# Kernel spectra of neighbouring time blocks added by accumulating transfers for all four sequences in six of eight channel chunks, with new places in the period and behind it

## The chip, the cores and the metric

The kernel runs on one core of a Trainium2 chip. The metric is the device time of one execution in microseconds (us); lower is better. The engines of the core are named as the profile names them: PE (TensorE, matrix products), DVE (VectorE, elementwise work), ACT (ScalarE, activations and copies), POOL (GpSimd, here mostly an issuer of transfers) and SP (SyncE, the other issuer of transfers).

## The reference

Two kinds of layer alternate, twice each, over `x` of 2048 rows and 512 channels:

```python
x = A_u
x = x + _A_ref(_layernorm(x), A_re, A_im, B_re, B_im, C_re, C_im, log_dt, Dskip)
x = x + _B_ref(_layernorm(x), w_gate, w_up, w_down)
x = x + _A_ref(...)          # the same parameters again
x = x + _B_ref(...)
# _A_ref: a long convolution per channel
dt = exp(log_dt); logdA = dt * (A_re + 1j*A_im); dB = dt * (B_re + 1j*B_im)
K = einsum("dn,dnl,dn->dl", C, exp(logdA[:, :, None] * arange(2048)), dB).real
y = irfft(rfft(u padded to 4096) * rfft(K padded to 4096))[:2048] + u * Dskip
# _B_ref: (silu(x @ w_gate) * (x @ w_up)) @ w_down, with 1376 hidden features
```

The filter `K` of each of the 512 channels has to be made once, from 128 complex exponentials per channel. Both convolution layers use it.

## The kernel before

The 2048 rows are cut into four blocks of 512 (`NB`). A convolution of blocks is done in the frequency domain: block `b` of the output needs, for every `k` up to `b`, the product of the spectrum of input block `b-k` with a kernel spectrum `w[k]`. A kernel spectrum `w[k]` covers two neighbouring time blocks of the filter, so for `k` of 1 to 3 it is a sum of two parts, one from the transform of block `k` and one, turned by a sign and with real and imaginary part exchanged, from that of block `k-1`. Each spectrum is taken as four sequences `q` of 128 frequencies. `w[0]` stays on the chip in `w0r`, the other three go to DRAM (`wdr`).

The filters are made in eight chunks of 64 channels. The work of the eight chunks overlaps in a repeating **period**, about 27 us long. For chunk `c` it holds, in the order in which one chunk passes through:

- `gen_tiles`, `gen_turns`, `gen_trig`, `gen_exp`: phases, sines, cosines and exponentials, written into `wall`, which holds two chunks in turn (DVE L409, L413, L417; ACT L428 to L430, L439 to L455). `upper` (ACT L449) squares a part of them into `mu`.
- `gen_g` and `gen_e`: the two factors of the filter (DVE L475 to L505 for `g`, L462 to L468 for the exponentials). The last step of `g` is an accumulating transfer issued by POOL (L495).
- `lags` (PE L515, 256 small products into the PSUM tile `pk`), then the copy `spread_in` (ACT L526), two transfers through DRAM that turn the layout round (SP L533 and L535) into the tile `kt`, and `skip` (DVE L522), which adds the direct term.
- `spectra(c, kt, q0)`, twice: for `q0` of 0 the sequences 0 and 2, for `q0` of 1 the sequences 1 and 3. Each does 16 fp32 products (32 records in the trace) into one of two large PSUM tiles (`pbig`) and makes the sums described above.
- `sizes` (ACT L625), beside it one spectrum of the second input block (`second`: PE L317, ACT L320, SP L321) and the norms of some weight rows (`weights`: POOL L348 loads, ACT L354 squares into `sq`, PE L357 sums, DVE L360 takes the largest). The loads use three buffers in turn, and each waits for the square that read its buffer before.

The two calls of `spectra` make the sum in two ways. With `q0` of 0, ACT copies the turned part to `wo` (L572), DVE adds the direct part from PSUM (L581), and SP stores the result. With `q0` of 1, ACT copies the turned part to `wo` and the direct part to `wa` (L576, tile tag `z`, one buffer), SP stores `wo`, and POOL then adds `wa` in DRAM with an accumulating transfer (`store_w(..., G, accum_op=OP.add)`, L556), which waits until the store has landed. Both also copy `w[0]` (L577).

The order of everything in the period is written by hand: `at(t, f)` puts a step on a list with a time, the list is sorted, and all instructions of PE, DVE, ACT and POOL are issued in that order (a step at a later number stands later in each engine's row; the number itself is not a time on the chip). `starts` gives the start of chunk `c`'s period, `n` in `use` is that of the next one. `prepare` places the phases and exponentials of a chunk two ahead, `factors` those of the next one. Behind the period comes a hand-written sequence of `take(...)` and `split(...)` calls: the last chunks' spectra (`first_parts`, `later_parts`), the first convolution (`conv`, `ssm_half`) and the split of the weights into two fp16 halves (`split`: ACT L681 and L706, DVE L679, L686 and L709). The rest, from about 296 us on, are the gated layers (`ffn`) beside the other convolutions; there a scheduler in the build sets the order.

Of the kernel before, what the change touches and what calls it, by code (L numbers as in the profile page):

```python
# [33 lines left out]
NCH = D // DC  # L34
# [43 lines left out]
def kernel(ctx, tc, x, a_re, a_im, b_re, b_im, c_re, c_im, log_dt, d_skip,  # L78
                           w_gate, w_up, w_down, c_ef, c_ei, c_ek, c_am, c_eh, c_eih, out):
    nc = tc.nc  # L80
    V, A, G, PE = nc.vector, nc.scalar, nc.gpsimd, nc.tensor
# [122 lines left out]
    def direct_size():  # L204

        da = tl([1, D], "da", "sg")
        A.activation(da, dsk, AF.Abs)
        V.tensor_reduce(dmax, da, axis=AX.X, op=OP.max)
# [238 lines left out]
    def upper(ts):  # L447

        A.activation(ts[2][:, 1:], ts[0][:, 1:32], AF.Square)  # L449
# [69 lines left out]
    def skip(ch, kt, eng):  # L519

        k = kt[0:1, :, 0]
        eng.tensor_tensor(k, k, dsk[:, ch * DC:(ch + 1) * DC].rearrange("p (g d) -> p g d", g=4), OP.add)  # L522
# [35 lines left out]
    def spectra(ch, kt, q0):  # L558


        h, cq = ch // NQ, ch % NQ
        pw = pbig([P, 2, 2, NB, 4, 16], "pw")
        for j in range(2):
            products(pw[:, j], kt, 0, NB, q0 + 2 * j, [(i, c) for i in range(2) for c in range(4)])
        yield
        if q0:
            wo = spare[0][:, 16 * DC:].rearrange("p (j k i d) -> p j k i d", j=2, k=NB - 1, i=2)
        else:
            wo = tl([P, 2, NB - 1, 2, DC], "wo", "sg")
        pv = pw.rearrange("p j i k g d -> p i j k (g d)")  # L570
        for i in range(2):
            A.activation(wo[:, :, :, i], pv[:, 1 - i, :, :NB - 1], AF.Copy, scale=sgn[:, i:i + 1])  # L572
        if q0:
            wa = tl([P, 2, NB - 1, 2, DC], "wa", "z")
            for i in range(2):
                A.activation(wa[:, :, :, i], pv[:, i, :, 1:], AF.Copy)  # L576
        A.activation(w0r[:, h, q0::2, cq], pw[:, :, :, 0].rearrange("p j i g d -> p j i (g d)"), AF.Copy)  # L577
        yield
        if not q0:
            wv = wo.rearrange("p j k i d -> p i j k d")  # L580
            V.tensor_tensor(wv, pv[:, :, :, 1:], wv, OP.add)  # L581
            yield
        for j in range(2):
            store_w(h, cq, q0 + 2 * j, wo[:, j])
        yield
        if q0:
            for j in range(2):
                store_w(h, cq, q0 + 2 * j, wa[:, j], G, accum_op=OP.add)
            yield
# [33 lines left out]
    def sizes(ch, kt, junk):  # L623

        A.activation(junk, kt, AF.Abs, accum_out=wsum[:, ch:ch + 1])  # L625
# [20 lines left out]
    def take(it, n):  # L646
        for _ in range(n):
            next(it, None)
# [332 lines left out]
    ts = [None] * (NCH + 2)  # L981
# [15 lines left out]
    with tc.manual_schedule(engines={mybir.EngineType.Activation, mybir.EngineType.DVE, mybir.EngineType.PE, mybir.EngineType.Pool}):  # L997
# [14 lines left out]
        tr = gen_trig(ts[0])  # L1012
# [10 lines left out]
        ge, tn = gen_e(ts[0]), gen_turns(1, ts[1])  # L1023
# [6 lines left out]
        tr = gen_trig(ts[1])  # L1030
# [24 lines left out]
        def at(t, f, n=1):  # L1055
            plan.append((t, len(plan), (lambda: take(f, n)) if hasattr(f, "__next__") else f))

        def later(make):

            yield from make()  # L1060

        def prepare(c, t):

            def tiles():
                ts[c] = gen_tiles(c)
            at(t + 0.05, tiles)
            steps = {k: later(lambda g=g: g(c, ts[c])) for k, g in
                     (("turns", gen_turns), ("exp", gen_exp))}
            tr = later(lambda: gen_trig(ts[c]))
            at(t + 0.35, steps["turns"])  # L1070
            at(t + 0.45, tr)
            at(t + 13.0, steps["turns"], 3)
            at(t + 13.2, steps["turns"], 3)
            at(t + 17.0, tr)
            at(t + 8.3, steps["exp"], 100)

        def factors(c, t):

            at(t + 0.2, lambda: upper(ts[c]))

            def tiles(c):
                gs[c] = tl([P, 2, 32, DC], "g", ("ga", "gb")[c % 2])
            if c == 1:
                at(t + 0.1, lambda: tiles(c))
            if c + 1 < NCH:
                at(t + 8.05, lambda: tiles(c + 1))
            gg, ge = later(lambda: gen_g(c, ts[c], gs[c])), later(lambda: gen_e(ts[c]))
            for k in range(4):
                at(t + 0.2 + 2 * k, gg, 2)
            at(t + 0.3, ge)  # L1090
            for k in range(5):
                at(t + 8.2 + k, gg)
            for k in range(4):
                at(t + 22.0 + 0.6 * k, ge, 1 if k < 3 else 100)

        def use(c, t):

            box, kt, n = {}, kt2[:, c % 2], starts[c + 1]

            def copy():  # L1100
                box["ks"] = spread_in(box["pk"])
                if c < NCH - 2:
                    spread(c, box["ks"], kt)
            at(t, lambda: box.update(pk=lags(ts[c], gs[c])))
            at(t + 7.1, copy)
            if c == NCH - 2:
                at(t + 10.0, lambda: spread_pe(c, box["ks"], kt))
            if c < NCH - 2:
                at(t + 13.1, lambda: skip(c, kt, V))
            at(t + 25.0, lambda: sizes(c, kt, box["ks"]))  # L1110
            for q0, ats in list(enumerate(((t + 17.5, t + 25.2, n + 2.1, n + 7.5),
                                      (n + 6.9, n + 14.0, n + 17.3, n + 21.0))))[:2 if c < NCH - 2 else 1]:
                sp = later(lambda q0=q0: spectra(c, kt, q0))
                if c == NCH - 2:
                    tail["sp"] = sp
                    ats = ats[:2]
                for t0 in ats:
                    at(t0, sp)

        def second_block(k, t):  # L1120
            box = []
            at(t - 3.0, lambda: box.append(second(*sec[k])))
            at(t + 14.0, lambda: take(box[0], 1))
            at(t + 17.6, lambda: take(box[0], 1))

        def weights(n, t0, t1, t2, t3):

# [19 lines left out]
        for i in range(NCH - 1):  # L1147
            t = starts[i]
            use(i, t)
            factors(i + 1, t)  # L1150
            second_block(i, t)
            if i + 2 < NCH:
                prepare(i + 2, t)
            for k, t0, t1, t2, t3 in ((0, -13.0, 0.25, 13.9, 22.3), (1, 0.3, 14.5, 17.45, 22.9),
                                      (2, 15.0, 26.5, 28.05, 36.0)):
                n = ((3, 3, 0), (3, 3, 0), (3, 3, 0), (3, 2, 0), (3, 2, 0), (3, 3, 0), (3, 3, 3))[i][k]
                if i == NCH - 2 and k == 2:
                    t0, t1, t2, t3 = 15.0, 20.0, 24.0, None
                if n:
                    weights(n, t + t0, t + t1, t + t2, t3 and t + t3)  # L1160
        t = starts[NCH - 1]
# [8 lines left out]
        c, kts = NCH - 1, (kt2[:, 0], kt2[:, 1])  # L1170
# [15 lines left out]
        def split(hi, lo, load=0):  # L1186
            for _ in range(load):
                loads.pop(0)()
            for _ in range(hi):
                his.pop(0)()  # L1190
            for _ in range(lo):
                los.pop(0)()
# [9 lines left out]
        conv = [ssm_half(0, 0, h) for h in range(2)]  # L1202
# [7 lines left out]
        ks = spread_in(pk)  # L1210
        odd = later_parts(c - 1, kts[0], (1, 3))
        rest = later_parts(c, kts[1])
# [4 lines left out]
        last = second(*sec[-1])  # L1217
# [15 lines left out]
        first_parts(c, 2)  # L1233
        take(conv[0], 1)
        split(1, 0)
        take(conv[1], 1)
        take(last, 1)
        take(last, 1)
        split(0, 1)
        split(0, 0, 1)  # L1240
        take(conv[1], 1)
        take(conv[0], 1)
        take(conv[1], 1)
        split(1, 0)
        split(1, 0)
        split(0, 0, 1)
# [8 lines left out]
        take(conv[1], 1)  # L1255
        take(odd, 1)
        direct_size()
        take(norm, 1)
        take(rest, 1)
        take(rest, 1)  # L1260
        take(odd, 1)
        take(conv[1], 1)
        take(rest, 1)
        take(odd, 1)
        take(block1, 1)
        take(rest, 1)
        split(1, 0)
        take(norm, 1)
        take(norm, 1)
        take(odd, 1)  # L1270
        take(rest, 1)
        split(0, 1)
        take(rest, 1)
        split(1, 0)
        take(rest, 1)
        split(0, 1)
        take(conv[0], 1)
        take(rest, 1)
        split(1, 0)
        take(rest, 1)  # L1280
        split(0, 1)
        split(0, 0, 1)
        split(0, 0, 1)
        take(rest, 1)
        split(0, 0, 1)
        take(rest, 1)
        sizes(c, kts[1], ks)
        take(rest, 1)
        nn2 = tl([P, 2, D], "nn2", "nn")
        nt3 = sb.tile([P, D], F16, name="nt3")  # L1290
        parts = itertools.cycle([nn2[:, 1].bitcast(F16)[:, i * D:(i + 1) * D] for i in range(2)] + [nt3])
# [54 lines left out]
```

## Time and profile before

| | |
|---|---|
| time, median of 3 runs (lowest to highest) | 1060.76 us (1058.98 to 1061.06) |
| the profiled execution: its own time, its span | 1060.34 us, 1058.3 us |
| share of the span: PE, DVE, ACT, POOL | 96%, 91%, 51%, 10% |
| mean granted PE clock | 0.99 |
| filters in the period (from the first `lags` to the last) | 52.6 to 249.5 us |
| hand-written sequence behind it | to about 296 us |
| gated layers and the other convolutions | 296 us to the end |

The profile is of one execution, taken on the chip. A row of the timeline reads: start, length, engine, line, operation, output and inputs, shapes, number of instructions in the row, and in brackets how long the engine stood idle before it and what released it. Rows of a group of instructions give the shortest, median and longest duration in ns. "issue" as a releaser is time in which the engine waited for nothing that the profile shows. The share of busy time is an average over stages with different limits, so each stage has to be read by itself.

### The profile page before, as it was taken

What the parts mean: (1) busy time and instruction counts of PE and PEld (TensorE: products, weight loads), DVE (VectorE), ACT (ScalarE), POOL (GpSimd) and SP (SyncE); (2) the same over time, 40 slices, a digit from 0 to 9 for tenths busy, and PEclk for the clock granted to TensorE, in tenths of its full rate; (3) what the DMA queues carried; (4) which work ended last, traced back from release to release, by engine and by line L of the source; (5) the groups of instructions that cost most, each with busy time, mean ns of one, the idle gap of its engine ahead of it and who ended that gap; (6) DMA issues with size and microseconds to landing.
All of it is one profiled execution on the core that took longest, in us unless ns stands there. A gap on an engine that the chain in (4) does not pass through costs nothing.

```text
span 1058.3 us, 21997 instructions
## 1 busy us (share of the span) xinstructions
PE 1011.4 (96%) x8934; PEld 797.8 (75%) x8934; DVE 960.8 (91%) x1372; ACT 543.1 (51%) x1093; POOL 108.0 (10%) x169
## 2 busy tenths in 40 slices
PE   2989999999899999999999999999999999999998
PEld 1868888888787868686877778686868778686775
DVE  8999999999899999999999999999999999995221
ACT  6989888863385346258454243532644262126210
POOL 1123322220000001011000000100010010000000
PEclk9989999999899999999999999999999999999999
DMA  6376777778765345241225544363342345321100
GB/s 219 114 194 161 166 174 186 192 190 269 245 224 145 105 120 146 98 147 34 53 89 144 177 150 155 93 152 101 106 150 78 122 125 152 110 84 44 22 26 20
DMA packets 120198, 139.73 MB, mean 132 GB/s; under 512 B 50705, under 2 KB 75793, under 8 KB 119330
## 3 DMA queue, kind: packets, MB, share of 16 engines
q1 hardware_dynamic: 108098, 112.83, 35.1%
q0 software_dynamic: 12000, 25.50, 10.3%
q8 instruction: 70, 1.15, 0.4%
q14 instruction: 30, 0.25, 0.1%
HBM read 91.36 MB, written 30.67 MB: 115 GB/s over the span
## 4 chain that ended last, share of the span: by engine, by line
PE 36%; DVE 27%; ACT 4%; DMA 3%; issue 3%; POOL 1%; SPq 0%; DVEq 0%; ACTq 0%
PE pgu L952 7%; PE pgu L953 7%; PE pgu L955 7%; DVE yk L835 4%; DVE t L832 4%; PE py L969 4%; PE py L968 4%; PE py L970 4%; DVE yk L832 3%; PE pi L804 2%; DVE sg L959 2%; DVE hl L961 1%; DVE z L245 1%; PE pf L293 1%; DVE fbt L245 1%
## 5 line engine op out<-in xcount | busy, mean ns | idle before, releaser
L952 PE MATMUL pgu<-mix,wall 128*128 128x256 f16 x1280 | 299.3, 273 | 3.8 <-DVE sg L959 2.0
L953 PE MATMUL pgu<-mix,wall 128*128 128x256 f16 x1280 | 299.3, 273 | 0.0
L955 PE MATMUL pgu<-mix,wall 128*128 128x256 f16 x1280 | 195.1, 273 | 0.3 <-DVE mix L893 0.3
L953 PEld LDWEIGHTS <-wall 128*128 128x128 f16 x1280 | 125.3, 98 | 20.3 <-issue 4.5
L952 PEld LDWEIGHTS <-wall 128*128 128x128 f16 x1280 | 125.1, 98 | 16.0 <-issue 0.3
L955 PEld LDWEIGHTS <-wall 128*128 128x128 f16 x1280 | 125.2, 98 | 15.1 <-issue 0.5
L968 PE MATMUL py<-wall,hh 128*128 128x512 f16 (+1 forms) x352 | 133.4, 379 | 0.0
L969 PE MATMUL py<-wall,hh 128*128 128x512 f16 (+1 forms) x352 | 133.4, 379 | 0.0
L970 PE MATMUL py<-wall,hl 128*128 128x512 f16 (+1 forms) x352 | 132.4, 379 | 0.0
L835 DVE TENSOR_TENSOR yk<-yk,t 128x1024 f32<-128x1024 f32 x96 | 117.4, 1223 | 0.3
L832 DVE TENSOR_TENSOR t<-uu,w 128x1024 f32<-128x1024 f32 x96 | 117.4, 1223 | 0.3
L960 ACT ACTIVATE hh<-sg 128x512 f16<-128x512 f32 x80 | 50.1, 627 | 125.8 <-DVE sg L959 125.8
L958 ACT ACTIVATE sg<-pgu,sc 128x512 f32<-128x512 f32 x80 | 54.4, 680 | 75.8 <-PE pgu L955 59.4
L553 PE MATMUL pw<-kt,ek 128*128 128x256 f32 (+1 forms) x384 | 91.2, 374 | 0.0
L959 DVE SCALAR_TENSOR_TENSOR sg<-pgu,sc,sg 128x512 f32<-128x512 f32 x80 | 60.0, 750 | 28.9 <-ACT sg L958 28.9
L553 PEld LDWEIGHTS pw<-kt,ek 128*128 128x128 f32 x384 | 72.7, 194 | 8.8
L961 DVE TENSOR_TENSOR hl<-sg,hh 128x512 f16<-128x512 f32 x80 | 55.2, 690 | 11.4 <-ACT hh L960 11.4
L970 PEld LDWEIGHTS <-hl 128*128 128x128 f16 (+1 forms) x352 | 34.3, 98 | 38.5
L969 PEld LDWEIGHTS <-hh 128*128 128x128 f16 (+1 forms) x352 | 34.4, 98 | 37.9
L968 PEld LDWEIGHTS <-hh 128*128 128x128 f16 (+1 forms) x352 | 34.4, 98 | 37.2
L515 PE MATMUL pk<-wall,g 128*32 128x64 f32 x2048 | 58.8, 287 | 2.0 <-issue 2.0
L515 PEld LDWEIGHTS pk<-wall,g 128*32 128x32 f32 x2048 | 56.0, 134 | 5.3 <-issue 5.3
(276 smaller groups left out, 1844.7 us busy)
## 6 DMA issues: line engine op xcount, KB each, us to landing
uu<-udr SPq DMA_DIRECT2D x96, 256.0 KB, 3.0
w<-wdr SPq DMA_DIRECT2D x96, 256.0 KB, 2.7
g<-g POOLq DMA_DIRECT2D x12, 512.0 KB, 7.1
udr<-u SPq DMA_DIRECT2D x16, 256.0 KB, 3.7
udr<-u POOLq DMA_DIRECT2D x16, 256.0 KB, 3.0
udr<-fbt POOLq DMA_DIRECT2D x16, 256.0 KB, 2.7
kdr<-ks SPq DMA_DIRECT2D x6, 512.0 KB, 3.1
kt<-kdr SPq DMA_DIRECT2D x24, 128.0 KB, 3.0
```

The costliest lines, as they stand in the source:

```text
L515: PE.matmul(pk[32 * grp:32 * grp + 32, dd, :], lhsT=g[:, i, :, d], rhs=e[:, 0:64, d], start=i == 0 and dd % 8 == 0, stop=i == 1 and dd % 8 ...
L553: PE.matmul(pw[:, i], lhsT=e, rhs=kt[:, :, c + 4 * k0:4 * k1:4, :].rearrange("p g k d -> p k g d"), start=c == 0, stop=c == 3)
L832: V.tensor_tensor(t, uu.unsqueeze(2).to_broadcast([P, NQ, 2, 2, DC]), w.unsqueeze(3).to_broadcast([P, NQ, 2, 2, DC]), OP.mult)
L835: V.tensor_tensor(yk, yk, t, OP.add)
L952: PE.matmul(o, lhsT=wgu(wi, k, 0)[:, fs], rhs=nh[:, k], start=k == 0, stop=False)
L953: PE.matmul(o, lhsT=wgu(wi, k, 1)[:, fs], rhs=nh[:, k], start=False, stop=False)
L955: PE.matmul(o, lhsT=wgu(wi, k, 0)[:, fs], rhs=nlo[:, k], start=False, stop=k == 3)
L959: V.scalar_tensor_tensor(sg, pgu[:, 1], sc6[:, 4:5], sg, OP.mult, OP.mult)
L961: V.tensor_tensor(hl[:, f0:f0 + 2], sg, hh[:, f0:f0 + 2], OP.subtract)
L968: PE.matmul(py[r], lhsT=hh[:n, f, rc], rhs=wd(f, 0)[:n], start=f == 0, stop=False)
L969: PE.matmul(py[r], lhsT=hh[:n, f, rc], rhs=wd(f, 1)[:n], start=False, stop=False)
L970: PE.matmul(py[r], lhsT=hl[:n, f, rc], rhs=wd(f, 0)[:n], start=False, stop=f == FT - 1)
```

## The change

In chunks 0 to 5 both calls of `spectra` now make the sum by an accumulating transfer; in chunk 6 the remaining call keeps the sum on DVE. `wa` is filled twice in a period, from one buffer. The steps `turns`, `tr`, `upper`, the last step of `second`, the steps of `spectra` and the squares of `weights` get other times, and the sequence behind the period is in another order.

```diff
@@ spectra
         h, cq = ch // NQ, ch % NQ
+        adds = ch < NCH - 2
...
-        if q0:
+        if adds:
             wa = tl([P, 2, NB - 1, 2, DC], "wa", "z")
...
-        if not q0:
+        if not adds:
             wv = wo.rearrange("p j k i d -> p i j k d")
             V.tensor_tensor(wv, pv[:, :, :, 1:], wv, OP.add)
...
-        if q0:
+        if adds:
             for j in range(2):
                 store_w(h, cq, q0 + 2 * j, wa[:, j], G, accum_op=OP.add)
@@ prepare
-            at(t + 13.0, steps["turns"], 3)
-            at(t + 13.2, steps["turns"], 3)
-            at(t + 17.0, tr)
+            at(t + 8.06, steps["turns"], 3)
+            at(t + 13.20, steps["turns"], 3)
+            at(t + 18.44, tr)
@@ factors
-            at(t + 0.2, lambda: upper(ts[c]))
+            at(t + 9.92, lambda: upper(ts[c]))
@@ use
-            for q0, ats in list(enumerate(((t + 17.5, t + 25.2, n + 2.1, n + 7.5),
-                                      (n + 6.9, n + 14.0, n + 17.3, n + 21.0))))[...]
+            for q0, ats in list(enumerate((((t + 17.50), (n + 0.40), (n + 0.50), (n + 1.56)),
+                                      (n + 6.90, n + 14.00, n + 14.20, n + 16.00))))[...]
@@ second_block
-            at(t + 17.6, lambda: take(box[0], 1))
+            at(t + 26.60, lambda: take(box[0], 1))
@@ weights (three groups of loads, squares, sums)
-            for k, t0, t1, t2, t3 in ((0, -13.0, 0.25, 13.9, 22.3), (1, 0.3, 14.5, 17.45, 22.9),
-                                      (2, 15.0, 26.5, 28.05, 36.0)):
+            for k, t0, t1, t2, t3 in ((0, -13.0, 2.10, 13.90, 22.3), (1, 0.3, 11.46, 17.45, 22.9),
+                                      (2, 15.0, 26.50, 31.06, 36.0)):
@@ the sequence behind the period (first of several moves of one step)
+        take(last, 1)
         take(conv[1], 1)
         take(last, 1)
-        take(last, 1)
         split(0, 1)
+        take(conv[1], 1)
         split(0, 0, 1)
         take(conv[1], 1)
         take(conv[0], 1)
-        take(conv[1], 1)
...
```

The names L572 and later are one line higher in the changed file (L576 of before is L577 there). Three places show how the rows move.

DVE, one period in the middle: `g` and `spare` are the steps of `gen_g`, `wall` with L413 and L417 the phases of `gen_turns`, `kt` the step `skip`.

```order
 L502 TENSOR_TENSOR spare<-g,xz 128x2x256
+L413 TENSOR_TENSOR wall<-tdk,am 128x128
+L417 ISA wall<-wall 128x256
+L417 ISA wall<-wall 128x512
 L505 TENSOR_TENSOR g<-g,spare 128x2x256
 L490 TENSOR_TENSOR g<-g,xz 128x2x512
```

The first three phase steps now stand ahead of the last two doublings of `g` and no longer behind the step L493; the step L581 is gone from the place after L409.

ACT, the first period (behind the copies `u` of the start): `xz` are the small phase tiles, `sq` the squares of the weights, `ks` the copy `spread_in`.

```order
-L449 ACTIVATE mu<-wall 128x1984
-L476 ACTIVATE xz<-xz 128x320
+L476 ACTIVATE xz<-xz 128x320
+L428 ACTIVATE xz<-xz 128x320
+L429 ACT_TABLE_LOAD
+L429 ACTIVATE xz<-xz 128x320
+L430 ACTIVATE xz<-xz,hpi 128x320
 L354 ACTIVATE sq<-st 128x512 x3
-L428 ACTIVATE xz<-xz 128x320
-L429 ACT_TABLE_LOAD
-L429 ACTIVATE xz<-xz 128x320
-L430 ACTIVATE xz<-xz,hpi 128x320
```

The three squares went behind the phase steps, right ahead of `ks`, and `mu` left this place for one behind the exponentials.

POOL, one period: `st` are the loads of weight rows, `g` the accumulating transfer of `gen_g`, `wdr<-wa` those of `spectra`.

```order
+L556 DMA wdr<-wa 128x3x128 x2
 L441 MEMSET wall 128x64
 L495 DMA g<-g 128x1024 x2
 L419 MEMSET wall 128x64
-L348 DMA st<-in_B_w_gate_dram 128x344 x3
 L556 DMA wdr<-wa 128x3x128 x2
-L348 DMA st<-in_B_w_gate_dram 128x344 x3
+L348 DMA st<-in_B_w_gate_dram 128x344 x6
```

A second pair of accumulating transfers stands ahead of the transfer of `g`, and the old pair moved ahead of three loads.

More of the change, by code (lines that the diff above doesn't have):

```diff
@@ L1071, in prepare @@
             at(t + 0.45, tr)
-            at(t + 13.0, steps["turns"], 3)
-            at(t + 13.2, steps["turns"], 3)
-            at(t + 17.0, tr)
-            at(t + 8.3, steps["exp"], 100)
+            at(t + 8.06, steps["turns"], 3)
+            at(t + 13.20, steps["turns"], 3)
+            at(t + 18.44, tr)
+            at(t + 8.30, steps["exp"], 100)
         def factors(c, t):
-            at(t + 0.2, lambda: upper(ts[c]))
+            at(t + 9.92, lambda: upper(ts[c]))
             def tiles(c):
@@ L1093, in factors @@
             for k in range(4):
-                at(t + 22.0 + 0.6 * k, ge, 1 if k < 3 else 100)
+                at(t + 22.00 + 0.60 * k, ge, 1 if k < 3 else 100)
         def use(c, t):
@@ L1104, in use @@
             at(t, lambda: box.update(pk=lags(ts[c], gs[c])))
-            at(t + 7.1, copy)
+            at(t + 7.10, copy)
             if c == NCH - 2:
@@ L1108, in use @@
             if c < NCH - 2:
-                at(t + 13.1, lambda: skip(c, kt, V))
-            at(t + 25.0, lambda: sizes(c, kt, box["ks"]))
-            for q0, ats in list(enumerate(((t + 17.5, t + 25.2, n + 2.1, n + 7.5),
-                                      (n + 6.9, n + 14.0, n + 17.3, n + 21.0))))[:2 if c < NCH - 2 else 1]:
+                at(t + 13.10, lambda: skip(c, kt, V))
+            at(t + 25.00, lambda: sizes(c, kt, box["ks"]))
+            for q0, ats in list(enumerate((((t + 17.50), (n + 0.40), (n + 0.50), (n + 1.56)),
+                                      (n + 6.90, n + 14.00, n + 14.20, n + 16.00))))[:2 if c < NCH - 2 else 1]:
                 sp = later(lambda q0=q0: spectra(c, kt, q0))
@@ L1122, in second_block @@
             at(t - 3.0, lambda: box.append(second(*sec[k])))
-            at(t + 14.0, lambda: take(box[0], 1))
-            at(t + 17.6, lambda: take(box[0], 1))
+            at(t + 14.00, lambda: take(box[0], 1))
+            at(t + 26.60, lambda: take(box[0], 1))
         def weights(n, t0, t1, t2, t3):
@@ L1257 @@
         direct_size()
+        take(rest, 1)
         take(norm, 1)
-        take(rest, 1)
         take(rest, 1)
@@ L1262 @@
         take(conv[1], 1)
+        split(1, 0)
         take(rest, 1)
@@ L1266 @@
         take(rest, 1)
-        split(1, 0)
         take(norm, 1)
@@ L1271 @@
         take(rest, 1)
+        take(rest, 1)
         split(0, 1)
-        take(rest, 1)
         split(1, 0)
@@ L1278 @@
         take(rest, 1)
+        take(rest, 1)
         split(1, 0)
-        take(rest, 1)
-        split(0, 1)
         split(0, 0, 1)
         split(0, 0, 1)
-        take(rest, 1)
         split(0, 0, 1)
@@ L1288 @@
         take(rest, 1)
+        take(rest, 1)
+        split(0, 1)
         nn2 = tl([P, 2, D], "nn2", "nn")
```

## The prediction

> **What bounds the kernel now.** First the page, for the shares and the queues.
>
> ```profile
> span 1058.3 us, 21997 instructions
> PE 1011.4 (96%) x8934; PEld 797.8 (75%) x8934; DVE 960.8 (91%) x1372; ACT 543.1 (51%) x1093; POOL 108.0 (10%) x169
> q0 software_dynamic: 12000, 25.50, 10.3%
> ```
>
> PE is busy for 96%, DVE for 91%: two engines share the bound, and only a view by stage tells who holds whom. So next the busy time in stretches of one period (columns: window, us, busy time and instructions of PE, PEld, DVE, ACT and POOL, granted clock, DMA share, GB/s).
>
> ```profile
> 164.00:191.00 27.00, 25.44 (x313) 22.35 (x317) 26.59 (x33) 24.11 (x55) 7.52 (x11) 0.94 0.77 182
> 191.00:218.00 27.00, 26.70 (x386) 23.51 (x379) 26.55 (x32) 24.23 (x56) 8.05 (x12) 1.00 0.81 192
> 400.00:600.00 200.00, 196.06 (x1558) 150.47 (x1556) 195.50 (x291) 98.28 (x190) 15.29 (x23) 1.00 0.37 109
> 600.00:800.00 200.00, 198.77 (x1585) 153.27 (x1583) 195.83 (x282) 88.59 (x173) 20.42 (x26) 1.00 0.44 129
> ```
>
> In the filters, of which two periods stand here, DVE is busy 26.6 of 27 us, PE 25.4 to 26.7, ACT 24. After 400 us PE holds the pace. Third, PE's timeline, where the start of `lags` (L515) marks a period:
>
> ```profile
> 79.84 7.25 PE L515 MATMUL pk<-wall,g 128*32 128x64 f32 x256
> 105.72 5.81 PE L515 MATMUL pk<-wall,g 128*32 128x64 f32 x201
> 132.24 7.25 PE L515 MATMUL pk<-wall,g 128*32 128x64 f32 x256
> 150.81 0.68 PE L357 MATMUL nrm<-sq,onesb 128*128 128x344 bf16 x2 [0.32 <-ACT sq L354]
> 152.34 0.67 PE L553 MATMUL pw<-kt,ef 128*128 128x256 f32 x2 [0.85 <-DVE kt L522]
> 159.42 4.39 PE L515 MATMUL pk<-wall,g 128*32 128x64 f32 x152
> 165.56 3.07 PE L515 MATMUL pk<-wall,g 128*32 128x64 f32 x104 [1.74 <-issue]
> 187.64 7.26 PE L515 MATMUL pk<-wall,g 128*32 128x64 f32 x256
> 206.63 0.67 PE L553 MATMUL pw<-kt,ef 128*128 128x256 f32 x2 [0.30 <-DVE kt L522]
> 242.23 7.26 PE L515 MATMUL pk<-wall,g 128*32 128x64 f32 x256
> 277.92 6.23 PE L804 MATMUL pi<-bb,mix 128*128 128x256 f32 x16 [4.27 <-DVE bb L851]
> ```
>
> Between 79.84 and 105.72 PE runs through: 25.88 us is what its work of a period takes. The period from 159.42 to 187.64 takes 28.22, and holds 1.74 us in which PE waits for nothing shown, at the lower clock of 0.94. Where PE waits for a named engine it is DVE's `skip` (0.85, 0.30), one square (0.32), and, in the sequence behind the period, DVE's sum for the convolution (4.27). Last, DVE's groups and its timeline in the period:
>
> ```profile
> L502 DVE TENSOR_TENSOR spare<-g,xz 128x1024 f32<-128x1024 f32 (+3 forms) x30 | 20.7, 691 | 1.1 <-ACT xz L476 1.1
> L581 DVE TENSOR_TENSOR wo<-pw,wo 128x768 f32<-128x768 f32 x7 | 6.7, 954 | 0.0
> 133.44 0.82 DVE L475 TENSOR_TENSOR xz<-xz,mz 128x640 f32<-128x640 f32 x1
> 134.58 2.29 DVE L462 TENSOR_TENSOR wall<-wall 128x2048 f32<-128x2048 f32 x1
> 137.19 0.95 DVE L581 TENSOR_TENSOR wo<-pw,wo 128x768 f32<-128x768 f32 x1
> 138.06 0.22 DVE L483 TENSOR_TENSOR g<-g,spare 128x64 f32<-128x64 f32 x1
> 141.54 0.68 DVE L502 TENSOR_TENSOR spare<-g,xz 128x512 f32<-128x512 f32 x1
> 151.05 0.28 DVE L413 TENSOR_TENSOR wall<-tdk,am 128x128 int32<-128x128 int32 x1
> 151.37 0.75 DVE L417 CUSTOM_DVE_ANT_0 wall<-wall 128x256 uint16<-128x256 uint16 x2
> 154.02 2.28 DVE L464 TENSOR_TENSOR wall<-wall 128x2048 f32<-128x2048 f32 x1
> ```
>
> The last two columns of a group are its busy time with the mean of one, and the idle time before it with what ended that. DVE's only waits of size are those of L502 for ACT's L476, 1.1 us together from 53 to 245 us.
>
> **The sum on DVE that goes.** Six of the seven L581 leave, those of chunks 0 to 5. One holds DVE from 137.19 to 138.06, so 0.87 each, 5.2 us. `upper` no longer stands ahead of L476 on ACT, so the three waits (1.1) should go too: 6.3 us is the most that DVE can win in the period.
>
> **How much of it PE can take.** From 79.84 to 187.64 four periods take 107.80, 26.95 each; four of 25.88 would be 103.5. So PE's room in them is 4.3 us, and 0.3 (the wait at 206.63) in the one after. Waits on named engines are 1.5 of these 4.6 (0.32, 0.85, 0.30). The period with the issue stall is 28.22 − 25.88 = 2.3 over; nothing in the edit acts on a stall of that kind, and whether it comes again is open, so I count half of it. DVE's period, with 0.87 and some 0.2 of waits less, falls from 26.95 to about 25.9, PE's own pace. So I take 4.6 − 1.2, about 3.3; the ends are the named waits alone (1.5) and the room (4.6). The last period (to 242.23) is full on PE; it carries the gain and adds none.
>
> **The first period.** There the squares move behind the small phase steps.
>
> ```profile
> 55.47 1.68 ACT L354 ACTIVATE sq<-st 128x512 bf16<-128x512 f32 x3
> 57.03 0.48 ACT L428 ACTIVATE xz<-xz 128x320 f32<-128x320 int32 x1
> 59.92 1.02 ACT L526 ACTIVATE ks<-pk 128x1024 f32<-128x1024 f32 x1 [0.16 <-PE pk L515]
> 70.73 1.22 PE L553 MATMUL pw<-kt,ef 128*128 128x256 f32 x2 [1.56 <-DVE kt L522]
> ```
>
> Before, the squares fill the time until L428 (57.03), which needs DVE's L409. Now ACT stands idle there, and the squares (1.6) push `ks` from 59.92 to about 61.3. The path from `ks` through the transfers and `skip` to PE at 70.73 has no other cover, so the first spectra start 1 to 1.4 us later; the second squares also go back by those 1.4 and by `upper` (1.9), and PE's sums of them stand ahead of the spectra. I take +1.1, from 0 (if loads or DVE hid it) to 1.4.
>
> **The added copies, stores and transfers.**
>
> ```profile
> 149.24 0.87 ACT L576 ACTIVATE wa<-pw 128x384 f32<-128x384 f32 x2
> 163.61 0.39 ACT L577 ACTIVATE w0r<-pw 128x256 f32<-128x256 f32 x1
> 154.27 3.35 POOL L556 DMA_DIRECT2D wdr<-wa  x2
> L556 POOL DMA_DIRECT2D wdr<-wa x12: 1349/2040/2566, 99.9 to 236.5; - x12
> DMA to landing us min/median/max: 7.8/9.3/10.3
> wdr<-wo SPq DMA_DIRECT2D x14, 192.0 KB, 2.9
> ```
>
> ACT gets two copies more (0.87 a period, 24.1 to 25.0 of about 26): 1 us of free time covers them, and without that cover the 0.87 would reach PE through `ks`. POOL, busy 8 of 27 us, issues two more transfers, 3.35 us a period. SP's store comes earlier, with no add ahead of it. The point is the one buffer of `wa`: the copies of the next call wait until both transfers have read it. From the end of a copy that is 2.9 (store landed), 1.35 (first issue) and 9.3 (landing), some 13.5 us; from the end of the copies at 149.24 (150.1) to the place of the other call's, beside `w0r` at 163.61, it is 13.5 as well. So ACT may wait about as often as not, by up to a microsecond, its free time. I take 0.1 us a period that gets through, 0.5 in all; the ends are 0 and the slow rival below. By the Trainium skill, page "DMA: Bandwidth & Descriptors", section "Anatomy of one DMA — SWDGE (gpsimd) path", a transfer of this kind takes about 2 us and its bytes by 436 KB a us, an estimate of 2.5 us for 192 KB. The rows say 7.8 to 10.3, so the measured value stands; by the page this term would be nil and the sum 0.5 lower.
>
> **The moved steps.** The first three steps of `turns` (151.05 and 151.37, about 1 us) stand ahead of the last doublings of `g`, and `skip` behind them as before, so DVE's work up to `skip` and up to the next `lags` is the same: 0. But L413 writes the half of `wall` that `lags` reads. At 151.05 `lags` (132.24, 7.25 long) had been done for 11.6 us; now L413 comes behind the L502 of 141.54, which is 8.8 us behind L475 (133.44), less the L581 and the wait for L476 7.6, at about 141.1: 1.6 us behind that end. Queued behind L413 is the rest of `g`, which the next `lags` needs, so a PE that is more than 1.6 us late, or a DVE that runs ahead as much, now stops DVE. Price: 0 while both keep step; beside the stall of 1.74 some 0.1; up to 1 us if DVE gets ahead. I take 0. The loads on POOL come 2 to 3 us later behind the `wa` pairs; their squares are needed half a period on, so nothing.
>
> **Behind the period.** DVE holds this sequence (PE's 4.27 for L851).
>
> ```profile
> 242.85 0.40 ACT L577 ACTIVATE w0r<-pw 128x256 f32<-128x256 f32 x1
> 244.06 0.95 DVE L581 TENSOR_TENSOR wo<-pw,wo 128x768 f32<-128x768 f32 x1
> ```
>
> Its operands are there 1.2 us before DVE reaches the L581 of chunk 6 (242.85 against 244.06), so DVE, which comes early by its own gain, can win those 1.2 more before inputs bind it; the new order lets PE's inverse transforms start beside the splits. I take 1.2, from −1 (a step of the new order that waits) to 2.5 (about half of the 4.27). The gated layers are scheduled anew in small pieces; PE stands idle 3.9 us in 400 to 600 against 1.2 in 600 to 800, so such a row can win or lose about 1.5: 0, plus or minus 1.5.
>
> **Sum.** −3.3 + 1.1 + 0.5 − 1.2 = −2.9 against the profiled execution's 1060.34, which is 0.4 under the median: 1057.4, say 1057.5. No change can be told from the measurement within 0.2%, 2.1 us: faster is below 1058.6, slower above 1062.9.
>
> **Rivals.**
> - *DVE's gain comes through whole.* The issue stall does not recur and waits don't couple: 6.3 in the period and 1.2 behind it, less 0.5: 1053.3. For it: DVE is at 98% in each period. Against it: it needs PE's period below its 25.88. Chance 0.15.
> - *PE holds the pace, nothing comes.* The named waits (1.5) are won, the first period loses 1.1, and the stall comes again, now stopping DVE too through L413, and the rest goes in small waits: 1059.5 to 1061. For it: PE is at 26.7 of 27 in one period already. 0.22.
> - *Slower: the one buffer of `wa`.* The twelve transfers (2.4 MB) add a tenth to the 25.5 MB of the software queue, at a DMA share of already 0.77 to 0.81. If landing slips from 9.3 by 2.5 us, ACT waits 2.5 a period, 1.5 beyond its free time, and with it `pw` and `ks`: in five periods 7.5, less a gain of 4: 1064. It decides when the transfers land over about 11 us from their issue, where wait and gain are even. 0.13.
> - *POOL's issuing blocks DVE.* Twelve more issues at 1.7 us (half of 3.35), if DVE stood still beside each, are 20 us: 1077. The rows speak against it: L464 took 2.28 while POOL issued at 154.27, the same operation on L462 2.29 at 134.58 with POOL idle. 0.02. The Trainium skill, page "SBUF — State Buffer", section "Who interferes with whom", calls the port pair that DVE shares with GpSimd an exclusive lock; these two rows show no such lock beside an issue.
>
> The forecast itself has 0.48; its own range is 1055.3 to 1059. That gives faster 0.43 + 0.15 = 0.58, same 0.05 + 0.22 = 0.27, slower 0.15. The range for 8 in 10 goes from the whole gain (1053) to a small loss (1062.5); most of the slow rival is left out.
>
> **What the new profile would show.** Right: L581 only for chunk 6; starts of `lags` 25.9 to 26.3 apart from the second on, the second about a microsecond later than 79.84; DVE without waits on L476; PE's waits on `skip` at 152 and 206 gone; `wa` landing within 10 us and ACT without waits of over 1 us for it; PE's wait before L804 near 4. Wrong: ACT idle ahead of the `wa` copies with a transfer as releaser; DVE idle before L413 with PE's `pk` as releaser; a period of 27 with DVE no longer full; the gain of the period given back behind 245 us, or in the gated layers by more than 1.5.

## The result, and the profile after

The changed kernel is slower: 1077.7 us median of 6 executions (1068.66 to 1085.59) against 1060.28 for the kernel before (1058.98 to 1061.27, 6 executions); the ratio is 1.0152, 95% interval 1.0125 to 1.0178. I had forecast 1057.5, in a range of 1053.0 to 1062.5, and had given "slower" 0.15. Here and below a median is over all executions, and a ratio leaves out those that the record counts as slow (1085.59 us here, 1085.02 in turns_back, 1076.91 and 1085.96 in first_and_turns). The profiled execution took 1074.51 us. Its page:

```profile
span 1072.5 us, 22011 instructions
PE 1016.6 (95%) x8934; PEld 800.5 (75%) x8934; DVE 956.2 (89%) x1366; ACT 548.7 (51%) x1105; POOL 128.2 (12%) x181
q0 software_dynamic: 16800, 27.86, 12.4%
```

The edit is there as written: DVE has six instructions and 4.6 us less, ACT twelve more, POOL twelve more transfers, and the software queue 2.4 MB more. The span is 14.2 us longer, of which PE is busy for 5.2; the rest went into waiting. The stretches of the period say where:

```profile
110.00:137.00 27.00, 25.09 (x310) 21.35 (x302) 24.75 (x31) 23.83 (x55) 9.19 (x14) 1.00 0.82 179
137.00:164.00 27.00, 24.42 (x280) 20.97 (x269) 23.81 (x28) 22.16 (x54) 9.88 (x15) 0.94 0.98 216
164.00:191.00 27.00, 25.38 (x339) 21.91 (x339) 24.32 (x32) 23.44 (x56) 10.16 (x13) 1.00 0.86 168
191.00:218.00 27.00, 24.10 (x328) 20.73 (x327) 23.06 (x29) 22.63 (x57) 10.75 (x14) 0.94 0.86 187
```

All three engines are less busy than in the two stretches of before that stand with the prediction: DVE 23.1 to 24.8 of 27 us (26.6 before), PE 24.1 to 25.4 (25.4 to 26.7), ACT 22.2 to 23.8 (24.1 to 24.2). No engine has become the bound; they wait for one another. From the first to the last `lags` 202.75 us pass (53.02 to 255.77) against 189.63 before, 13.1 of the 14.2 us. The view of the waits between 50 and 260 us names what they wait for (columns: engine, tile and line that waited, what released it, us in total, times, longest):

```profile
POOL wdr L556 <- DMA wdr<-spare: 38.4, 7, 8.5
ACT wa L577 <- DMA wdr<-wa: 21.8, 5, 6.3
DVE kt L522 <- DMA kt<-kdr: 9.3, 4, 3.6
PE pw L553 <- ACT w0r L578: 6.1, 5, 1.8
PE pw L553 <- DMA kt<-kdr: 2.7, 3, 1.1
DVE wall L413 <- PE pk L515: 2.6, 4, 1.3
```

None of the six was there before; of PE's, the 2.7 us for `kt` stand in place of 2.7 us for `skip`. One period of the timeline shows them as one chain, in order of time (rows of ACT, SP, POOL, PE and DVE):

```profile
127.69 0.86 ACT L577 ACTIVATE wa<-pw 128x384 f32<-128x384 f32 x2
127.81 1.70 SPq L556 DMA_DIRECT2D wdr<-spare  x2
135.20 2.57 POOL L556 DMA_DIRECT2D wdr<-wa  x2 [8.44 <-DMA wdr<-spare]
137.59 1.03 ACT L573 ACTIVATE wo<-pw,am 128x384 f32<-128x384 f32 x2
143.34 0.87 ACT L577 ACTIVATE wa<-pw 128x384 f32<-128x384 f32 x2 [4.72 <-DMA wdr<-wa]
144.54 1.22 PE L553 MATMUL pw<-kt,ef 128*128 128x256 f32 x2 [1.74 <-ACT w0r L578]
146.84 1.00 ACT L526 ACTIVATE ks<-pk 128x1024 f32<-128x1024 f32 x1
147.87 0.33 SPq L533 DMA_DIRECT2D kdr<-ks  x1
155.28 0.21 DVE L522 TENSOR_TENSOR kt<-kt,tdk 1x64 f32<-1x64 f32 x1 [2.58 <-DMA kt<-kdr]
158.12 0.67 PE L553 MATMUL pw<-kt,ef 128*128 128x256 f32 x2 [0.77 <-DVE wall L417]
```

The second call fills `wa` until 128.55. Its accumulating transfers wait for the store of `spare` and are issued at 135.20, and they have read `wa` only when ACT's wait at 143.34 ends. The first call of the next chunk stands ready to write `wa` at 138.62, and ACT stops for 4.72 us, since it works in order. Behind it on ACT stand `w0r`, which frees the PSUM tile for PE's next spectra (1.74), and `ks`, from which `kt` is made: `skip` on DVE then waits 2.58 us for `kt`, and all of DVE with it. The waits of `skip` are new because `kt` now comes late.

### The profile page after: what moved, and what is told of

The parts are those of the page before. It is cut to its first block, busy times and chain, and to the rows that moved or that the text cites. A ratio compares the mean times of both kernels' runs of the same rounds, so it can differ in the third digit from the quotient of the medians.

```text
span 1072.5 us, 22011 instructions
## 1 busy us (share of the span) xinstructions
PE 1016.6 (95%) x8934; PEld 800.5 (75%) x8934; DVE 956.2 (89%) x1366; ACT 548.7 (51%) x1105; POOL 128.2 (12%) x181
## 5 line engine op out<-in xcount | busy, mean ns | idle before, releaser
L553 PE MATMUL pw<-kt,ek 128*128 128x256 f32 (+1 forms) x384 | 94.0, 383 | 0.0
```

The costliest lines, as they stand in the source:

```text
L553: PE.matmul(pw[:, i], lhsT=e, rhs=kt[:, :, c + 4 * k0:4 * k1:4, :].rearrange("p g k d -> p k g d"), start=c == 0, stop=c == 3)
```

## The experiments

The table gives each kernel's ratio to the kernel before, and from its profiled execution: its time, the stretch from the first to the last start of `lags`, and the stretch from there to the first product of the gated layers.

| kernel | ratio, 95% interval | profiled, us | first to last `lags`, us | then to the gated layers, us |
|---|---|---|---|---|
| before | 1 | 1060.34 | 189.63 | 53.03 |
| changed | 1.0152 (1.0125 to 1.0178) | 1074.51 | 202.75 | 51.79 |
| three_buffers | 1.0055 (1.0029 to 1.0081) | 1065.64 | 190.73 | 56.56 |
| three_z6 | 1.0043 (1.0022 to 1.0064) | 1062.45 | 191.75 | 52.15 |
| three_old_tail | 0.9985 (0.9971 to 1.0000) | 1060.04 | 191.40 | 52.21 |
| adds_old_times | 1.0085 (1.0065 to 1.0105) | 1071.31 | 198.59 | 54.03 |
| times_alone | 1.0013 (0.9999 to 1.0028) | 1065.20 | 193.60 | 53.06 |
| transfers_alone | 1.0015 (1.0002 to 1.0029) | 1064.67 | 190.38 | 53.12 |

**The buffer, the times or the traffic.** Three theories: the one buffer of `wa`, the moved steps by themselves, or the added traffic whatever the buffer. The first kernel takes the wait away without a tile more, by dealing out the three tiles that the calls have anyway:

```diff
-        if q0:
+        if adds and not q0:
             wo = spare[0][...]
         else:
-            wo = tl([P, 2, NB - 1, 2, DC], "wo", "sg")
+            wo = tl([P, 2, NB - 1, 2, DC], "wo", "z" if q0 else "sg")
...
-            wa = tl([P, 2, NB - 1, 2, DC], "wa", "z")
+            wa = tl([P, 2, NB - 1, 2, DC], "wa", "sg" if q0 else "z")
```

> The changed kernel, with the buffers of the two calls dealt out anew and none added: the first call takes `spare` for wo and tag z for wa, the second tag z for wo and tag sg for wa, so a wa has a whole period until its buffer is written again. Buffer theory (ACT stands still for wa's transfers, 21.8 us in five waits, and with it ks, kt and the spectra): these waits go, the periods fall from 28 to 32 us to about 26 to 27, and the time to 1056 to 1061. Traffic theory (twelve more accumulating transfers slow the transfers of kt and the stores, whatever the buffer): kt still lands 1 to 3 us late, 1068 or more. Times theory (the moved steps themselves cost): 1068 or more, with ACT idle elsewhere.

Measured: 1065.82 us, between the 1056 to 1061 of the buffer theory and the 1068 of the two others. The period is back at 190.7 us, as the buffer theory has it. Behind it the profiled execution took 3.5 us longer, where my own edit had added a wait: chunk 6's `wo`, in `sg`, had to wait 4.3 us for chunk 5's last `wa`.

The sum alone in the kernel before (`if q0` replaced by `if adds` in three places, nothing moved):

> The kernel before, in which only the sum is changed: both calls use wa and the accumulating transfers in chunks 0 to 5, all times and the sequence behind the period as before. Buffer theory: the gap between the copies is the same and the transfers are issued later (behind three loads), so ACT waits as long or longer: 1072 to 1085. Traffic theory: about 1072 to 1078. Times theory: 1055 to 1061.

Measured: 1070.85 us, below my range but slower without any moved step, which the times theory excludes; between the two others it does not decide. Two waits of this kernel:

```profile
DVE spare L502 <- ACT xz L476: 16.4, 6, 3.5
ACT wa L577 <- DMA wdr<-wa: 5.1, 5, 1.8
```

Here the buffer's wait is small, and the loss has another way: copies, `upper` and the wait stand on ACT ahead of L476, and DVE pays 16.4 us at L502. So the sum costs time at the old places as well, but not by the same wait.

The moves without the sum:

```diff
-        adds = ch < NCH - 2
+        adds = q0
```

> The changed kernel with its times and its sequence behind the period, but with the sum of the first call on DVE in every chunk, as before. Buffer and traffic theory: no 12 transfers and no second use of wa, so about the time before, 1057 to 1062. Times theory: 1068 or more.

Measured: 1062.93 us, 0.9 above the range that the buffer and the traffic theory had given it, and at most 0.3% above before by its interval. The moved steps are not what costs 17 us.

The traffic without the buffer:

```diff
+        elif ch < NCH - 2:
+            for j in range(2):
+                G.dma_start(xtra[ch, j]..., ek[0]...[:, 384 * j:384 * (j + 1)]..., accum_op=OP.add)
```

> The kernel before, with all its times and DVE's sum, and 12 more accumulating transfers of 192 KB (two a period, at the place of the store of the first call) from constants that nothing writes again into DRAM that nothing reads: the traffic and the issuing without the buffer. Buffer theory: 1060 to 1063. Traffic theory: kt lands late and DVE waits for it, 1068 or more. Times theory: 1060 to 1062.

Measured: 1063.17 us, 0.2 above the range of the buffer theory; the ratio is 1.0015, its interval just clear of 1. By the ratio the twelve transfers cost 1.6 us, not 17, and the transfers of `kt` landed after 3.1 us (3.0 before), so not late.

**The buffer apart from the sequence behind the period.** First the wait that three_buffers had added is taken away, then also the old sequence behind the period, and then the changed kernel with only that old sequence:

```diff
 (three_z6, three_old_tail)
-            wo = tl([P, 2, NB - 1, 2, DC], "wo", "z" if q0 else "sg")
+            wo = tl([P, 2, NB - 1, 2, DC], "wo", "z")
 (three_old_tail, one_buffer_old_tail: all from `c, kts = NCH - 1, ...` on as before)
```

> The changed kernel with the three buffers dealt out as in three_buffers, and chunk 6's wo in tag z instead of sg, where it had waited 4.3 us for chunk 5's last accumulating transfer and kept DVE's L582 standing 6.1 us. Buffer theory: this wait was the one buffer's last effect; L582 then has its operands near 243 and the time falls by 3 to 4 us from 1065.8 to 1061 to 1063, the rest above before being the later first period and the moved steps. Rival, the new sequence behind the period costs that by itself: 1065 again.

> three_z6 with the hand-written sequence behind the period as in the kernel before. If the new sequence is worth something or costs something by itself, this differs from three_z6 by it: theory that it is neutral, within 1.5 us of three_z6; rival that it costs, 3 us or more below three_z6.

> The changed kernel, its one buffer of wa as it is, with only the hand-written sequence behind the period as in the kernel before. Buffer theory: the waits on wa stay (some 20 us in five or six), the periods stay at 28 to 32 us, and the time at 1070 to 1078; against three_old_tail (1059.7), which differs in the buffers alone, 12 us or more. Rival, the new sequence behind the period is what costs: 1063 or less.

Measured: 1064.71, 1059.65 and 1075.06 us (the last a ratio of 1.0138, 1.0112 to 1.0164; first to last `lags` 202.52 us). With the old sequence the buffers alone decide between 1.0138 and 0.9985, 1.5% of the time; with the new one between 1.0152 and 1.0043, 1.1%. So the buffers are the cause of 1.1 of the 1.5% with the new sequence, and of all of the loss with the old one. In the waits, one_buffer_old_tail above and three_old_tail below:

```profile
ACT wa L577 <- DMA wdr<-wa: 17.9, 5, 5.4
DVE kt L522 <- DMA kt<-kdr: 7.3, 3, 3.6
```

```profile
PE nrm L357 <- ACT sq L354: 7.3, 3, 5.4
DVE kt L522 <- DMA kt<-kdr: 2.1, 2, 1.8
```

The wait for `wa` is gone, and with it most of the wait of `skip`, though the transfers of `kt` land after 4.0 us in both kernels: late `kt` was for the most part the consequence of the wait for `wa`.

three_z6 stays 0.4% above before. I had expected 1061 to 1063 of it, and 1065 if the new sequence costs by itself; 1064.71 speaks for the second, and so does three_old_tail, 5.1 us below it where I had set 3 or more if the new sequence costs. Without the added wait the stretch behind the period fell from 56.56 to 52.15 us in the profiled executions, but the ratio only from 1.0055 to 1.0043, which the intervals do not tell apart. The 0.58% between three_z6 and three_old_tail I can't place. In the profiled executions the sequence behind the period takes the same time (52.15 and 52.21 us), and three_z6 was profiled in one of its shorter executions (1062.45 of a median of 1064.71). The granted clock was lower in the executions of three_z6 (0.983 to 0.994, against 0.989 to 0.995); whether that is a cause or a consequence is not shown. With one buffer the two sequences differ by only 0.14%, inside the intervals. So a cost of the new sequence is measured with three buffers alone, and by what it comes is open.

**The old places with three buffers.** adds_old_times with the buffers of three_z6, and then with `upper` at its new place:

```diff
 (old_times_three_upper alone)
-            at(t + 0.2, lambda: upper(ts[c]))
+            at(t + 9.92, lambda: upper(ts[c]))
```

> adds_old_times (1070.9) with the three buffers of three_z6. There DVE stood 16.4 us for ACT's L476 and ACT 5.1 us for the transfers of wa. Buffer theory: the copies' wait goes and with it a part of the waits on L476: 1062 to 1066. If instead L476 is late because the copies and the squares of upper stand ahead of it, the 16 us on DVE mostly stay: 1068 or more.

> old_times_three with only upper (L449) at its new time, behind the exponentials, so that L476 stands 1.9 us earlier on ACT. If the gain of the six sums on DVE can be had at all, it is here: waits on L476 under 2 us, periods near 26.3 and 1056 to 1059. If PE's own pace or the traffic takes it: 1060 to 1063.

Measured: 1068.34 us (1.0072, 1.0055 to 1.0089) and 1067.19 us (1.0057, 1.0042 to 1.0072); first to last `lags` 197.87 and 195.11 us. The first came out as I had set it for an L476 that is late because of what stands ahead of it. But it does not test the old places without a wait for the buffer: there the new deal only moves the wait, from the copies of `wa` (5.1 us) to those of `wo` at L573, which in the second call now have the tile of the first call's `wa` (5.7 us in four, and 2.5 us in the second kernel). The waits for L476 fell from 16.4 to 12.2 and then to 2.1 us, but by the ratios only 1.4 and 3.0 us of time came back. The second missed my range by 4 us. At the old places PE's waits for the squares are 9.8 us and DVE waits 3.7 us for ACT's L430 (3.8 and none before), but three_old_tail has 7.3 and 0.8 us of the same waits, so this can be a part of the reason at most. The sum does need the new places, 0.9985 against 1.0057; which of the steps beside `upper` it needs is not shown.

**What is left of the gain.** Without the wait for the buffer the kernel with the old sequence gained 0.15%, its interval reaching 1, where I had forecast 0.3%, and the period had not become shorter at all. What the six sums are worth was then measured alone, in the kernel before:

```diff
-            V.tensor_tensor(wv, pv[:, :, :, 1:], wv, OP.add)
+            if ch == NCH - 2:
+                V.tensor_tensor(wv, pv[:, :, :, 1:], wv, OP.add)
```

> The kernel before, with the six DVE sums L581 of chunks 0 to 5 left out and nothing put in their place (the spectra of sequences 0 and 2 lack the direct part): what the sums are worth on DVE, without copies, transfers or moves. If my term held (3.3, between 1.5 and 4.6, and 1.2 behind the period at most): 1055 to 1058.5. If the sums are hidden beside PE and ACT in the period: 1059.5 to 1061.

Measured: 1061.91 us, a ratio of 1.0003 (0.9988 to 1.0019). Six sums of 0.87 us gone and nothing put in their place, and the time is the same, 0.9 us above the range that I had set for sums hidden beside PE and ACT. The wait view says why, first of the kernel before and then of this one:

```profile
ACT wall L428 <- DVE wall L417: 16.1, 6, 4.0
DVE spare L502 <- ACT xz L476: 1.1, 3, 0.6
```

```profile
ACT wall L428 <- DVE wall L417: 16.0, 6, 4.1
DVE spare L502 <- ACT xz L476: 6.0, 6, 1.5
```

The wait of L502 grew by 4.9 of the 5.2 us, while ACT's wait at L428 stayed as it was. That is a ring: ACT waits at L428 for DVE's L417, works without a pause from there to L476, and DVE waits for that at L502. The sum stands on DVE between L417 and L502, beside ACT's row, and had only filled a part of the wait.

Then the new places, three buffers, and the twelve added transfers left out:

```diff
-            for j in range(2):
+            for j in range(2 if q0 else 0):
                 store_w(h, cq, q0 + 2 * j, wa[:, j], G, accum_op=OP.add)
```

> three_old_tail (1059.7) with the twelve added accumulating transfers left out, and with them the direct part of sequences 0 and 2; copies, buffers and times are the same. DMA engines are busy for 0.93 to 0.99 of the time in three periods of three_old_tail. If the traffic eats the gain of the sums there: kt's waits go, the first to the last lags take 188 us or less, and the time is 1055 to 1057.5. If not, and PE and the moved steps bound it: 1059 to 1060.5.

Measured: 1062.78 us (1.0017, 1.0000 to 1.0033), first to last `lags` 189.98 us. DVE's and PE's waits for `kt` are gone, and those on L476 too, yet nothing is gained over before. Three of the waits of PE and DVE that are left:

```profile
PE nrm L357 <- ACT sq L354: 7.3, 3, 5.4
PE pk L515 <- issue: 2.2, 3, 1.1
DVE wall L413 <- PE pk L515: 1.6, 2, 0.9
```

The 5.4 us stand in the first period (3.5 before). From 80 to 242 us DVE is busy for 154.7 us, 3.7 less than before, but PE for 158.6 of the 162 us (158.3 before). I read this as PE now holding the pace there; no run tests it. The traffic isn't what eats the gain. This kernel came out 2.3 us above the range that I had set and above three_old_tail, which does more. The profiled execution was 1.2 us shorter than that of three_old_tail, both at a granted clock of 0.992, and the other executions ran at 0.986 to 0.992 against 0.989 to 0.995; why is open.

**Two moved steps put back**, in three_old_tail: the squares of the first period (`2.10 if i else 0.25`), the first steps of `turns` (`t + 13.0`), and both.

> three_old_tail with the three squares of the first period back at 0.25, ahead of the small phase steps, the other periods unchanged. If the first period lost time by them as the prediction put it (1.1, from 0 to 1.4): the start of the second lags comes 0.6 to 1.4 us earlier against the first, and the time is 1058.5 to 1059. If the upper squares (L449) ahead of the second squares hold PE instead: no change of the time.

> three_old_tail with the first three steps of turns back behind L493. DVE's waits of L413 for lags (1.9 us) go. If the move was free, as the prediction put it, no change beyond 1 us: 1059 to 1060.5. If it helps, since skip no longer stands ready while kt is on its way: 1 us or more above three_old_tail; if its wait cost, 1058 or less.

> three_old_tail with both repairs: the first period's squares and the first three steps of turns at their old places. The two kernels with one of them were at 1058.9 and 1059.9 (medians). If they add: 1057.5 to 1058.5, and first to last lags about 188 to 189 us. If the traffic or PE binds: 1058.5 to 1060.

Measured: 1058.95 us (0.9986, 0.9969 to 1.0003), 1059.89 us (1.0010, 0.9984 to 1.0036) and 1059.35 us (0.9983, 0.9969 to 0.9996). The starts of the first and second `lags` in three_old_tail, and then in first_squares:

```profile
52.63 7.25 PE L515 MATMUL pk<-wall,g 128*32 128x64 f32 x256
80.41 7.25 PE L515 MATMUL pk<-wall,g 128*32 128x64 f32 x256
```

```profile
51.85 7.25 PE L515 MATMUL pk<-wall,g 128*32 128x64 f32 x256
79.03 7.25 PE L515 MATMUL pk<-wall,g 128*32 128x64 f32 x256
```

The first period falls from 27.78 to 27.18 us (27.24 before), so the squares cost 0.6 us there. In time no one of the three differs from three_old_tail by more than the intervals; the ratio of turns_back is lifted above 1 by three executions of 1068 to 1071 us. In first_and_turns the 188.44 us from the first to the last `lags` came as I had set them for two moves that add, 1.2 less than before, but its time fell into the other range. It has the lowest ratio, and as the only one of the fourteen experiments an interval wholly below 1: 0.17% faster than the kernel before (0.04 to 0.31).

## Why the prediction was wrong, step by step

- **The buffer (taken at 0.5 us in all, measured 1.1 to 1.5% of the time).** This is the step that failed. I compared 13.5 us that the buffer is held with 13.5 us between the copies, and found them even. The first was about right, though its parts were not: from the end of the copies (128.55) the pair was issued 6.65 us later and the buffer was free at 143.34, 14.8 us in all. The second I took from the places of before (150.1 to 163.61). In that gap ACT had done two squares and had then stood idle for 3.00 us:

```profile
150.24 0.89 ACT L354 ACTIVATE sq<-st 128x344 bf16<-128x344 f32 x2
154.14 1.91 ACT L428 ACTIVATE wall<-wall 128x2048 f32<-128x2048 int32 x1 [3.00 <-DVE wall L417]
```

  In the changed kernel `upper` and a group of squares stand ahead of the second call's copies. They put these off by about as much as ACT had waited behind them, so the gap loses its idle time and its squares:

```profile
123.87 1.84 ACT L449 ACTIVATE mu<-wall 128x1984 f32<-128x1984 f32 x1
125.62 1.23 ACT L354 ACTIVATE sq<-st 128x344 bf16<-128x344 f32 x3
128.69 1.93 ACT L428 ACTIVATE wall<-wall 128x2048 f32<-128x2048 int32 x1
```

  The first call is ready at 138.62, 10.1 us later and not 13.5, and so it is in each of the five periods in which ACT waited. I had listed both moves and did not carry them into this difference. adds_old_times, with the sum at the old places, bears this out: ACT's six waits at L428 are still 17.7 us there, the gap is 13.6 us (125.28 to 138.89), and the five waits for `wa` are 0.69 to 1.79 us, close to the "up to a microsecond" that I had worked out for these places.
- **The price of that wait.** I let ACT's free microsecond cover it, and had the rival cost 1.5 us a period beyond that. Five waits of 3.05 to 6.34 us went through ACT's order into `ks`, `kt` and `skip`, and stopped DVE for 9.3 us and PE for 6.1 at `w0r`; PE's 2.7 at `kt` are no more than its 2.7 at `skip` before. Three of the signs that I had named for a wrong forecast came: ACT idle ahead of the copies of `wa` with a transfer as releaser, DVE idle before L413, and a period of 27 us and more with DVE no longer full.
- **The rival's condition.** The slow rival named the right buffer, and set 1064 for it if the transfers landed 11.8 us from their issue, with wait and gain even at 11. They landed after 6.4 (median), faster than the 9.3 of before; it was the store ahead of them that took longer:

```profile
wdr<-wa POOLq DMA_DIRECT2D x24, 192.0 KB, 6.4
kt<-kdr SPq DMA_DIRECT2D x24, 128.0 KB, 4.1
wdr<-spare SPq DMA_DIRECT2D x12, 192.0 KB, 6.9
```

  The store of `spare` went from 2.3 to 6.9 us. It now starts behind the two transfers of `g` and no longer ahead of them (127.81 against 124.84 in the period above; before 149.37 against 151.44). That this is why it took longer is not shown; in times_alone, without the added transfers, it stands behind them too and took 5.0 us, and in transfers_alone 3.1. By the Trainium skill, page "DMA: Bandwidth & Descriptors", section "Anatomy of one DMA — SWDGE (gpsimd) path", the transfers of `wa` were estimated at 2.5 us; the rows, 4.2 to 7.8 us with a median of 6.4, again say more. A condition on one leg of a chain was the wrong test; the sum of the legs against the gap was the right one.
- **The sums on DVE (taken at 3.3 us of 6.3).** The instructions went as forecast. But the room on PE that I let them fill was made of waits and stalls, and sums_left_out shows that without them the old order takes 0.3 us more (from 1.3 less to 2.0 more by the interval). In the new order the waits on L476 do go, and three_without_transfers still takes 189.98 us for the period against 189.63. Of the 3.3 us the most that any kernel of the record shows is the 1.2 us by which the period of first_and_turns is shorter, in one profiled execution.
- **The first period (+1.1).** Right in place and cause, and 0.8 in size: 28.05 us against 27.24, and 0.6 us come back when the squares do.
- **`turns` and L413 (0).** The wait came as described, 2.6 us in four. turns_back shows no difference in time that its interval could tell.
- **Behind the period (−1.2).** In the changed kernel the stretch is 1.2 us shorter (51.79 against 53.03), but DVE did not come early: it stood 5.7 us at the last sum, L582, for a `w0r` that stood behind ACT's waits. So the number agrees by luck. Against that, executions of three_z6 and three_old_tail say that the new sequence costs 0.58%, which the profiles don't show.
- **POOL's issuing and DVE.** The rival had 0.02, and the trace after speaks against it again: an operation like the two compared before took the same 2.28 us beside POOL's issue at 135.20.

```profile
136.21 2.28 DVE L462 TENSOR_TENSOR wall<-wall 128x2048 f32<-128x2048 f32 x1
```

## What to carry to other kernels

When a change uses a buffer twice as often, write down for each use when it is filled and when its last reader is done, with the steps where the change puts them, and follow the whole chain of readers (the copy, the store, the wait on another queue, the issue, the landing); a microsecond too little stops an engine that works in order, and everything behind it. A gap that is read from the old trace can hold idle time that the change itself takes away, as the 3.00 us at L428 here. A packed engine is not by that a bound: before work is taken from it at a price, leave the work out once and see whether the time falls, for here 5.2 us of DVE's work only filled a wait. And when three tiles are at hand, deal them out by how long each use holds its tile; that alone moved 1.1 to 1.5% here.

## What was not expected of the hardware

The changed kernel's times spread far more than those of before: its executions took 1068.66 us at a mean granted PE clock of 0.991 and 1084.15 us at 0.977, while 25 executions of the kernel before, at 0.988 to 0.993, lay between 1058.8 and 1063.5. Why was not tested. And the DMA engines were busy for 0.93 to 0.99 of three stretches of three_old_tail without `kt` landing much later than in the changed kernel (4.0 and 4.1 us; 3.0 before, where the share was 0.77 and 0.81 in the two stretches shown). One of the three:

```profile
164.00:191.00 27.00, 26.27 (x373) 23.13 (x369) 26.56 (x32) 25.98 (x60) 11.59 (x15) 1.00 0.98 188
```
